# Weights cast by software-queue DMAs into place, and u transposed by DMAs on ScalarE's queue, in a fused retention and low-rank-mixer kernel

## The chip, the cores and the metric

The kernel runs on one core of one Trainium2 chip. The metric is the device time of one execution in microseconds (us); the kernel before takes 255.03 us (median of 3 runs, 253.96 to 255.19). Runs called slow (over 1.5% above the fastest of the same kernel) are left out of the ratios that are quoted.

## The reference

```python
# q, k, v: (4, 8, 768, 64); U: (768, 32); V: (32, 768); w_ch1: (512, 2048); w_ch2: (2048, 512); all fp32
state = 0                                        # per batch and head
for t in range(768):                             # retention
    state = gamma[h] * state + outer(k[t], v[t])
    y[t]  = (q[t] @ state) / 8
x  = heads of y side by side                     # (4, 768, 512)
u  = x + (x.T @ U @ V).T                         # low-rank mixing over the sequence
out = u + relu(u @ w_ch1) @ w_ch2                # MLP, "up" and "down"
```

The kernel computes the recurrence in six chunks of 128 positions, as masked scores plus a carried state ("attention" below). The MLP is nearly all of the TensorE (PE) work.

## The kernel before

The core treats batch 0's attention first and then works in four stages. In stage b the MLP of batch b runs while the attention of batch b+1, and its low-rank mixing, are woven between the MLP's matmuls at fixed marks (fractions of the MLP's work). The up half needs u transposed (uT, 512 features on partitions); the down half needs the MLP's hidden gT and w2.

```python
def prep_w1(mb, engines="PPPP"):        # w1: loaded as fp32 by SP (SyncE), cast to bf16 on POOL (GpSimd)
    for c in range(NCB):
        cast(engines[c], w1b[:, c, ts(mb, 512)], take("w1", mb, c))
        feed_more()                      # issues the next load of SP's list

def load_w2(j):                          # w2: cast by the software-queue DMA itself
    nc.gpsimd.dma_start(out=w2b[:, ds(4 * j, 4)],
        in_=moe_w_ch2[ds(512 * j, 512)].rearrange("(m p) n -> p m n", p=P))

def lr_turn(b, j0, eng="A"):             # u turned on TensorE, two blocks of 128 rows at a time
    r = R[j0 // 2 % 2]
    for c in range(NCB):
        for jj in range(2):
            nc.tensor.matmul(r[:, c // 2, ds(256 * (c % 2) + P * jj, P)],
                             us[b][:, j0 + jj, ts(c, P)], ident, start=True, stop=True)
    evac(eng, uTs[b][:, :, ds(j0 * P, 2 * P)], r.rearrange("p n (c t) -> p (n c) t", c=2))
# ... cut: attention, projection, up and down pieces ...
for ci in range(3): prep_turned("k", 1, ci)      # POOL, in this order
load_w2(0); load_w2(1)
for ci in range(3): prep_turned("q", 1, ci)
load_w2(2); load_w2(3)
# ... cut ...
AT = {1: at(0.44, 0.075, 0.037), 2: at(0.09, 0.105, 0.05)}             # attention marks
LR = {1: (0.89, 0.92, 0.945, 0.97), 2: (0.71, 0.75, 0.83, 0.89)}       # mix, expand, turn 0-1, turn 2-3
```

`evac` is an eviction: it copies the result of matmuls to the place where the next step reads it. Blocks 4 and 5 of a batch are turned early in the next stage (marks 0.06 to 0.10), because only the second part of the up half needs them. Blocks 0 to 3 are turned at the border between stages, because the very first up matmul needs all four.

Of the kernel before, what the change touches and what calls it, by code (L numbers as in the profile page):

```python
# [9 lines left out]
fp32 = mybir.dt.float32  # L10
# [6 lines left out]
def kernel(  # L17
# [11 lines left out]
    nc = tc.nc  # L29
    P = 128  # L30
    B, H, S, D = q.shape
    NCK = S // P
    DM = H * D
    RK = moe_U.shape[1]
    DH = moe_w_ch1.shape[1]
    NM = DH // P
    NCB = DM // P
# [8 lines left out]
    wts = ctx.enter_context(tc.tile_pool(name="wts", bufs=1))  # L46
    rin = ctx.enter_context(tc.tile_pool(name="rin", bufs=RING))
    rinT = ctx.enter_context(tc.tile_pool(name="rinT", bufs=1))
# [11 lines left out]
    R = [psum.tile([P, 2, 512], fp32, tag="r0", name="r0")]  # L60
# [12 lines left out]
    def evac(eng, dst, src):  # L73
        if eng == "A":
            nc.scalar.activation(dst, src, AF.Copy)  # L75
        else:
            nc.vector.tensor_copy(out=dst, in_=src)

    def cast(eng, dst, src, scale=None):
        if eng == "A":  # L80
            assert scale is None
            nc.scalar.activation(dst, src, AF.Copy)
            return
        e = nc.vector if eng == "D" else nc.gpsimd
        if scale is None:
            e.tensor_copy(out=dst, in_=src)  # L86
        else:
            e.tensor_tensor(dst, src, scale, op=ALU.mult)  # L88

    Ub = wts.tile([P, NCK, RK], bf16)  # L90
    V4 = wts.tile([P, S], bf16)
    w1b = wts.tile([P, NCB, DH], bf16)
    w2b = wts.tile([P, NM, DM], bf16)
    Vf = wts.tile([P, S], fp32)

    feed = []
    n_fed, n_used, n_held = [0], [0], [0]
# [4 lines left out]
    def feed_natural(nm, b, ci):  # L102
        src = {"q": q, "k": k, "v": v}[nm]
        feed.append(((nm, b, ci),
                     src[b, :, ts(ci, P), :].rearrange("h p d -> p h d")))
# [5 lines left out]
    def load_whole(nm, b):  # L111
        open_in(nm, b)
        src = {"q": q, "k": k}[nm][b]
        for hp in (0, 2, 1, 3):
            nc.sync.dma_start(  # L115
                out=turned_in[nm, b][ds(32 * hp, 32)].rearrange(
                    "p h c x -> p (h c) x"),
                in_=src[ds(2 * hp, 2)].rearrange("h (c t j) d -> t (h c) (j d)",
                                                 c=NCK, t=32))

    def feed_more():
        while n_fed[0] < len(feed) and n_held[0] < RING:
            key, src = feed[n_fed[0]]
            if key[0] == "T" and n_cast[key[1] - 1] < 2 * NCK:
                return
            n_fed[0] += 1
            if key[0] == "T":
                load_whole("k", key[1])
                load_whole("q", key[1])
                continue  # L130
            if key[0] == "V":
                for c in range(NCB):
                    nc.sync.dma_start(out=Vf[ds(RK * c, RK)], in_=src)
                continue
            n_held[0] += 1
            t = rin.tile([P, 512], fp32, tag="in", name=f"in_{n_fed[0]}")
            ready[key] = t
            if key[0] == "U":
                t = t[:, :NCK * RK].rearrange("p (j r) -> p j r", j=NCK)
            elif key[0] in "qkv":  # L140
                t = t.rearrange("p (h d) -> p h d", h=H)
            nc.sync.dma_start(out=t, in_=src)  # L142

    def take(*key):
        n_held[0] -= 1
        return ready.pop(key)

    for ci in range(NCK):
        for nm in "qkv":
            feed_natural(nm, 0, ci)  # L150
    feed.append((("U",), moe_U.rearrange("(j p) r -> p j r", p=P)))
    feed.append((("V",), moe_V))
    for mb in range(4):
        for c in range(NCB):
            feed.append((("w1", mb, c), moe_w_ch1[ts(c, P), ts(mb, 512)]))
    for b in range(1, B):
        feed.append((("T", b), None))
        for ci in range(NCK):
# [25 lines left out]
    for h in range(H):  # L184
        r = ds(32 * (h // 2), 32)
# [6 lines left out]
    ident = consts.tile([P, P], bf16)  # L192
# [4 lines left out]
    for i in range(NST):  # L197
        t = consts.tile([P, 4, P], bf16, name=f"state{i}")
# [34 lines left out]
            prep_natural("k", b, ci)  # L233
        prep_natural("v", b, ci)

    def prep_uv(eng):
        cast(eng, Ub.rearrange("p j r -> p (j r)"), take("U")[:, :NCK * RK])
        feed_more()
        cast(eng, V4, Vf)

    def prep_w1(mb, engines="PPPP"):
        for c in range(NCB):
            cast(engines[c], w1b[:, c, ts(mb, 512)], take("w1", mb, c))
            feed_more()

    def load_w2(j):
        nc.gpsimd.dma_start(
            out=w2b[:, ds(4 * j, 4)],
            in_=moe_w_ch2[ds(512 * j, 512)].rearrange("(m p) n -> p m n", p=P))
# [5 lines left out]
    def open_x(b):  # L255
        xs[b] = xp.tile([P, NCK, DM], bf16, tag="x", name=f"x_{b}")
# [99 lines left out]
    us, uTs, pcs = {}, {}, {}  # L356
# [27 lines left out]
                R[g][:, :, :nj * P].rearrange("p c (j e) -> p c j e", j=nj),  # L384
                v4(xs[b][:, ds(j0, nj), e]), op=ALU.add)

    def lr_turn(b, j0, eng="A"):
        r = R[j0 // 2 % 2]
        for c in range(NCB):
            for jj in range(2):  # L390
                nc.tensor.matmul(r[:, c // 2, ds(256 * (c % 2) + P * jj, P)],  # L391
                                 us[b][:, j0 + jj, ts(c, P)], ident, start=True,
                                 stop=True)
        evac(eng, uTs[b][:, :, ds(j0 * P, 2 * P)],
             r.rearrange("p n (c t) -> p (n c) t", c=2))


    stores = []

# [68 lines left out]
    def part(f, *args):  # L468
        return lambda: f(*args)


    def prep_first(ci):
        for nm, tag, g in (("q", "qi", gq), ("k", "kd", gk), ("v", "vd", None)):
            t = rpre.tile([P, H, D], bf16, tag=tag, name=f"{nm}d_0_{ci}")
            src = take(nm, 0, ci).rearrange("p (h d) -> p h d", h=H)
            if g is not None:
                g = g[:, ci, :, None].to_broadcast([P, H, D])
            cast("P", t, src, g)
            pre[nm, 0, ci] = t
            feed_more()  # L480
# [59 lines left out]
    def x_turn(j, cs):  # L540
        for c in cs:
            if c not in xT:
                xT[c] = bank("mlp" if c < 3 else "qk")
            nc.tensor.matmul(xT[c][:, ts(j, P)], xs[0][:, j, ts(c, P)], ident,
                             start=(j == 0), stop=False, skip_group_check=True)

    with tc.tile_pool(name="psum0", bufs=1, space=bass.MemoryType.PSUM) as psum0:
        open_x(0)
        prep_first(0)
        for ci in range(NCK):  # L550
            turn0(ci)
            if ci + 1 < NCK:
                prep_first(ci + 1)
            else:
                prep_uv("P")
            if ci > 0:
                mix0(ci - 1)
            score0(ci)
            if 0 < ci <= NLO:
                x_turn(ci - 1, range(3))  # L560
        n_cast[0] = 2 * NCK
        for mb in range(4):
            prep_w1(mb)
        for j in range(NLO):
            x_turn(j, (3,))
        mix0(NCK - 1)
        lr_open(0)
        p_p = bank("o")
        for j in range(NCK):
            for c in range(NCB):  # L570
                nc.tensor.matmul(p_p[ds(RK * c, RK), :P], Ub[:, j],
                                 xs[0][:, j, ts(c, P)], start=(j == 0),
                                 stop=(j == NCK - 1))
        pcs[0] = rmid.tile([P, P], bf16, tag="pc", name="pc_0")
        evac("D", pcs[0], p_p[:, :P])
        for c in range(NCB):
            nc.tensor.matmul(xT[c][:, :LO], pcs[0][ds(RK * c, RK)],
                             V4[ds(RK * c, RK), :LO], start=False, stop=True,
                             skip_group_check=True)
        for c in range(NCB):  # L580
            evac("AD"[c % 2], uTs[0][:, c, :LO], xT[c][:, :LO])
# [2 lines left out]
    R.append(psum1.tile([P, 2, 512], fp32, tag="r1", name="r1"))  # L584
    for ci in range(3):
        prep_turned("k", 1, ci)
    load_w2(0)
    load_w2(1)
    for ci in range(3):
        prep_turned("q", 1, ci)  # L590
    load_w2(2)
    load_w2(3)
    for ci in range(3):
        prep_natural("v", 1, ci)

    def at(b0, dc, dm):
        return [(b0 + dc * ci, b0 + dc * ci + dm) for ci in range(NCK)]

    AT = {1: at(0.44, 0.075, 0.037), 2: at(0.09, 0.105, 0.05)}
    LR = {1: (0.89, 0.92, 0.945, 0.97), 2: (0.71, 0.75, 0.83, 0.89)}  # L600
    for b in range(1, B):
        w = min(b, 2)
        if b > 1:
# [2 lines left out]
        else:  # L606
            marks = [(0.03, part(lr_expand, 0, 4, 2)), (0.10, part(lr_turn, 0, 4)),
                     (0.16, part(lr_expand, 0, 0, 4))]
        step = AT[w][1][0] - AT[w][0][0]
        for ci in range(NCK):  # L610
            s_at, m_at = AT[w][ci]
            marks.append((s_at - 0.6 * step, part(turn_chunk, b, ci)))
# [7 lines left out]
        def mixed():  # L620
            lr_open(b)
            lr_proj(b)
        marks += zip(LR[w], (mixed, part(lr_expand, b, 0, 4), part(lr_turn, b, 0),
                             part(lr_turn, b, 2)))
        weave(mlp_pieces(b - 1), marks)
    b = B - 1
# [32 lines left out]
```

## Time and profile before

The four stages, from the first up matmul of a batch to that of the next (from the timeline of PE):

| | first up matmul | stage 0 | stage 1 | stage 2 | stage 3 |
|---|---|---|---|---|---|
| before, us | 32.55 | 69.16 | 51.34 | 51.92 | 47.73 |

Stages 0 and 1 hold the same kinds of work, so stage 0 is about 18 us too long. The view by windows shows it, with stages 0 to 2 as its rows. The columns are the stretch, its length, then the busy time of PE, PE's weight load, DVE (VectorE), ACT (ScalarE), POOL (with instruction counts), the granted PE clock, the mean share of 16 DMA engines (it can come out above 1), and GB/s:

```profile
32.55:101.71 69.16, 59.42 (x637) 31.60 (x637) 27.63 (x49) 22.41 (x48) 34.80 (x46) 0.91 1.05 220
101.71:153.05 51.34, 51.21 (x600) 27.35 (x600) 24.65 (x45) 19.13 (x42) 27.71 (x37) 1.00 0.89 193
153.05:204.97 51.92, 51.26 (x601) 27.43 (x600) 24.98 (x45) 19.12 (x42) 13.16 (x18) 1.00 0.09 32
```

In stages 1 and 2 PE is busy almost without a gap at full clock. In stage 0 PE idles for 9.7 us and runs at a mean clock of 0.91. The table of waits of PE names the reasons (total us, times, longest):

```profile
PE r L314 <- DVE qT L264: 5.8, 1, 5.8
...
PE mlp L437 <- DMA w2b<-in_moe_w_ch_dram: 1.2, 1, 1.2
PE r L391 <- DVE u L382: 1.1, 2, 0.7
PE mlp L414 <- ACT uT L75: 0.9, 2, 0.7
```

The first line is the turned q of batch 1, which comes late from memory. The last two are what turning u on PE costs at the borders, beside the matmuls themselves. The timeline of POOL shows why w2 is late too: its DMAs stand behind casts that wait for k and q (in brackets, the idle time before and what ended it).

```profile
51.70 2.11 POOL L86 CAST ki<-kin 128x512 bf16<-128x512 f32 x3 [6.90 <-DMA kin<-in_k_dram]
53.73 1.70 POOL L247 DMA_DIRECT2D w2b<-in_moe_w_ch_dram  x2
58.52 3.04 POOL L88 TENSOR_TENSOR qi<-qin,gqT 128x512 bf16<-128x512 f32 x3 [3.10 <-DMA qin<-in_q_dram]
61.51 1.56 POOL L247 DMA_DIRECT2D w2b<-in_moe_w_ch_dram  x2
```

The border of stage 0 to 1, from the chain of waits (start, duration, what):

```profile
97.62 1.23 DVE u L382
...
99.28 0.86 PE mlp L437 x4
100.15 0.46 PE r L391 x8
...
100.63 1.03 ACT uT L75
...
101.71 1.02 PE mlp L414 x4
```

From the last piece of u (98.85) to the first matmul that uses uT (101.71) it is 2.9 us, and PE fills part of it with other work (the down matmuls, L437).

### The profile page before, as it was taken

What the parts mean: (1) busy time and instruction counts of PE and PEld (TensorE: products, weight loads), DVE (VectorE), ACT (ScalarE), POOL (GpSimd) and SP (SyncE); (2) the same over time, 40 slices, a digit from 0 to 9 for tenths busy, and PEclk for the clock granted to TensorE, in tenths of its full rate; (3) what the DMA queues carried; (4) which work ended last, traced back from release to release, by engine and by line L of the source; (5) the groups of instructions that cost most, each with busy time, mean ns of one, the idle gap of its engine ahead of it and who ended that gap; (6) DMA issues with size and microseconds to landing.
All of it is one profiled execution on the core that took longest, in us unless ns stands there. A gap on an engine that the chain in (4) does not pass through costs nothing.

```text
span 252.7 us, 5495 instructions
## 1 busy us (share of the span) xinstructions
PE 221.9 (88%) x2304; PEld 122.7 (49%) x2304; DVE 102.6 (41%) x193; ACT 87.6 (35%) x182; POOL 100.0 (40%) x138
## 2 busy tenths in 40 slices
PE   0784789954889998999999999999999999999991
PEld 0573534543545544445754454447644544584440
DVE  5433344413147434566544525556544242221121
ACT  3556335441323312555541033556410315450000
POOL 4776565057765207994108815720001010000110
PEclk9999779996599999999999999999999999999998
DMA  8999899999958999957999932000011120001211
GB/s 158 218 218 191 247 350 256 217 211 212 208 97 176 266 233 205 228 148 167 207 206 218 263 109 86 0 4 4 0 44 64 65 83 0 3 0 41 86 62 63
DMA packets 66857, 35.45 MB, mean 140 GB/s; under 512 B 51856, under 2 KB 63120, under 8 KB 66832
## 3 DMA queue, kind: packets, MB, share of 16 engines
q1 hardware_dynamic: 62800, 26.71, 52.1%
q0 software_dynamic: 4032, 8.39, 11.9%
q8 instruction: 18, 0.29, 0.5%
q14 instruction: 7, 0.06, 0.1%
HBM read 30.90 MB, written 6.29 MB: 147 GB/s over the span
## 4 chain that ended last, share of the span: by engine, by line
PE 45%; issue 20%; DMA 16%; SPq 10%; POOL 3%; DVE 2%; ACT 1%; POOLq 0%; DVEq 0%; ACTq 0%
PE mlp L437 21%; PE mlp L414 16%; SPq L142 9%; DMA in<-in_moe_w_ch_dram 5%; DMA qin<-in_q_dram 5%; DMA w2b<-in_moe_w_ch_dram 4%; PE r L347 2%; PE r L314 2%; POOL out_dram L403 2%; DMA Vf<-in_moe_V_dram 2%; SPq L115 1%; PE r L338 1%; DVE a L320 1%; PE r L391 1%; PE st L299 1%
## 5 line engine op out<-in xcount | busy, mean ns | idle before, releaser
L414 PE MATMUL mlp<-uT,w1b 128*128 128x512 bf16 (+1 forms) x512 | 92.3, 335 | 1.7 <-ACT uT L75 0.9
L437 PE MATMUL mlp<-w2b,gT 128*128 128x512 bf16 x384 | 89.5, 382 | 1.2 <-DMA w2b<-in_moe_w_ch_dram 1.2
L414 PEld LDWEIGHTS <-w1b 128*128 128x128 bf16 x512 | 49.4, 100 | 34.7 <-issue 3.7
L421 ACT ACTIVATE gT<-mlp 128x512 bf16<-128x512 f32 (+1 forms) x88 | 42.7, 490 | 53.6 <-PE mlp L414 52.7
L437 PEld LDWEIGHTS <-gT 128*128 128x128 bf16 x384 | 35.7, 98 | 40.7 <-issue 1.8
L403 POOL DMA_DIRECT2D out_dram<-o x24 | 13.3, 555 | 89.5 <-DVE o L442 89.5
L442 DVE TENSOR_TENSOR o<-mlp,u 128x512 f32<-128x512 f32 x24 | 16.6, 692 | 50.0 <-PE mlp L437 50.0
L419 DVE TENSOR_SCALAR gT<-mlp 128x512 bf16<-128x512 f32 (+1 forms) x40 | 22.0, 552 | 34.8 <-PE mlp L414 34.8
L320 DVE TENSOR_TENSOR a<-r,mask 128x512 bf16<-128x512 f32 x36 | 23.2, 685 | 18.8 <-PE r L314 17.1
L88 POOL TENSOR_TENSOR qi<-qin,gqT 128x512 bf16<-128x512 f32 x18 | 18.7, 1045 | 20.0 <-DMA qin<-in_q_dram 20.0
L75 ACT ACTIVATE x<-r 128x256 bf16<-128x256 f32 x36 | 11.8, 381 | 28.9 <-PE r L347 28.7
L88 POOL TENSOR_TENSOR vd<-in,gk 128x512 bf16<-128x512 f32 x18 | 18.7, 1043 | 7.8 <-DMA in<-in_v_dram 4.6
L75 ACT ACTIVATE uT<-r 128x1024 bf16<-128x1024 f32 x10 | 10.2, 1022 | 28.0 <-PE r L391 28.0
L86 POOL CAST ki<-kin 128x512 bf16<-128x512 f32 x18 | 13.5, 761 | 14.5 <-DMA kin<-in_k_dram 14.5
L382 DVE TENSOR_TENSOR u<-r,x 128x512 bf16<-128x512 f32 (+1 forms) x16 | 14.6, 952 | 6.6 <-PE r L375 6.6
L520 DVE TENSOR_TENSOR a<-r,mask 128x512 bf16<-128x512 f32 x12 | 7.7, 686 | 14.1 <-PE r L515 14.1
L314 PE MATMUL r<-qT,kT 32*128 32x128 bf16 x288 | 7.6, 225 | 5.8 <-DVE qT L264 5.8
L86 POOL CAST w1b<-in 128x512 bf16<-128x512 f32 x16 | 9.8, 613 | 5.5 <-DMA in<-in_moe_w_ch_dram 5.1
L314 PEld LDWEIGHTS <-kT 32*128 32x128 bf16 x288 | 4.5, 96 | 11.5 <-issue 10.3
L264 DVE STREAM_TRANSPOSE qT<-qi 128x256 f32<-128x256 f32 x18 | 7.3, 406 | 6.7 <-POOL qi L88 6.7
L489 PE MATMUL qk<-ident,qd 128*128 128x128 bf16 x24 | 3.5, 295 | 6.5 <-DVE ident L193 6.5
L75 ACT ACTIVATE qkT<-qk 128x1024 bf16<-128x1024 bf16 x6 | 6.1, 1024 | 8.7 <-PE qk L491 8.7
(70 smaller groups left out, 147.5 us busy)
## 6 DMA issues: line engine op xcount, KB each, us to landing
in<-in_v_dram SPq DMA_DIRECT2D x24, 256.0 KB, 5.7
out_dram<-o POOLq DMA_DIRECT2D x24, 256.0 KB, 2.6
in<-in_k_dram SPq DMA_DIRECT2D x18, 256.0 KB, 5.5
kin<-in_k_dram SPq DMA_DIRECT2D x12, 384.0 KB, 7.8
qin<-in_q_dram SPq DMA_DIRECT2D x12, 384.0 KB, 13.0
in<-in_moe_w_ch_dram SPq DMA_DIRECT2D x16, 256.0 KB, 6.2
w2b<-in_moe_w_ch_dram POOLq DMA_DIRECT2D x4, 512.0 KB, 9.9
in<-in_q_dram SPq DMA_DIRECT2D x6, 256.0 KB, 5.2
```

Source lines behind the costliest of these rows:

```text
L75: nc.scalar.activation(dst, src, AF.Copy)
L86: e.tensor_copy(out=dst, in_=src)
L88: e.tensor_tensor(dst, src, scale, op=ALU.mult)
L142: nc.sync.dma_start(out=t, in_=src)
L314: nc.tensor.matmul(R[hp // 2][:, hp % 2, ts(i, P)], turned("kT", b, ci, i, c, r), turned("qT", b, ci, i, c, r), start=(c == 0), stop=(c == 1))
L320: nc.vector.tensor_tensor(a[:, ds(4 * g, 4)].rearrange("p (n i) m -> p n i m", n=2), R[g][:, :, :256].rearrange("p n (i m) -> p n i m", i= ...
L403: nc.gpsimd.dma_start(out=dst, in_=src)
L414: nc.tensor.matmul(g_p[:, :sz], w1b[:, c, ts(m, P)], uTs[b][:, c, ds(lo, sz)], start=(c == 0), stop=(c == NCB - 1))
L419: nc.vector.tensor_relu(gT[:, m, ds(lo, sz)], g_p[:, :sz])
L421: nc.scalar.activation(gT[:, m, ds(lo, sz)], g_p[:, :sz], AF.Relu)
L437: nc.tensor.matmul(ch, gT[:, m, ts(j, P)], w2b[:, m], start=(m == 0), stop=(m == NM - 1))
L442: nc.vector.tensor_tensor(o_sb, ch, us[b][:, j], op=ALU.add)
```

## The change

Its intent: take the casts of w1, U and V off POOL by letting the software-queue DMA cast while it loads; load w2 early, behind w1; load k, q of batch 1 after w1 and beside w2 (a dummy POOL copy from w1's last column, the gate, holds them back); and take the transposes of u off PE and ScalarE.

```diff
-    def prep_w1(mb, engines="PPPP"): ...      (and prep_uv, Vf, the w1/U/V loads on SP)
+    def load_u():    nc.gpsimd.dma_start(out=Ub, in_=moe_U.rearrange("(j p) r -> p j r", p=P))
+    def load_v(c):   nc.gpsimd.dma_start(out=V4[ds(RK * c, RK)], in_=moe_V)
+    def load_w1(mb):
+        nc.gpsimd.dma_start(out=w1b[:, :, ts(mb, 512)],
+            in_=moe_w_ch1[:, ts(mb, 512)].rearrange("(c p) n -> p c n", p=P))
 ...
-    def lr_turn(b, j0, eng="A"):  (8 matmuls with ident, one eviction)
+    def lr_turn(b, j0):
+        for j in (j0, j0 + 1):
+            nc.scalar.dma_start(out=uTs[b][:, :, ts(j, P)], in_=us[b][:, j], transpose=True)
 ...
             turn0(ci)
             if ci + 1 < NCK:
+                if ci == NCK - 2:
+                    load_w1(0)
+                    load_w1(1)
                 prep_first(ci + 1)
+                if ci == 0:  load_u()
+                elif ci < 3: load_v(2 * ci - 2); load_v(2 * ci - 1)
 ...
+        load_w1(2); load_w1(3)
+        for j in range(4): load_w2(j)
+        gate = rinT.tile([P, 2, NCK, 256], fp32, tag="kin", name="gate")
+        nc.gpsimd.tensor_copy(out=gate[:1, 0, 0, :1], in_=w1b[:1, 0, DH - 1:])
         n_cast[0] = 2 * NCK
+        feed_more()
 ...
-    AT = {1: at(0.44, 0.075, 0.037), ...
-    LR = {1: (0.89, 0.92, 0.945, 0.97), ...
+    AT = {1: at(0.56, 0.052, 0.026), ...
+    LR = {1: (0.87, 0.89, 0.905, 0.905), ...
```

More of the change, by code (lines that the diff above doesn't have):

```diff
@@ L93 @@
     w2b = wts.tile([P, NM, DM], bf16)
-    Vf = wts.tile([P, S], fp32)
     feed = []
@@ L130, in feed_more @@
                 continue
-            if key[0] == "V":
-                for c in range(NCB):
-                    nc.sync.dma_start(out=Vf[ds(RK * c, RK)], in_=src)
-                continue
             n_held[0] += 1
@@ L137, in feed_more @@
             ready[key] = t
-            if key[0] == "U":
-                t = t[:, :NCK * RK].rearrange("p (j r) -> p j r", j=NCK)
-            elif key[0] in "qkv":
-                t = t.rearrange("p (h d) -> p h d", h=H)
-            nc.sync.dma_start(out=t, in_=src)
+            nc.sync.dma_start(out=t.rearrange("p (h d) -> p h d", h=H), in_=src)
     def take(*key):
@@ L150 @@
             feed_natural(nm, 0, ci)
-    feed.append((("U",), moe_U.rearrange("(j p) r -> p j r", p=P)))
-    feed.append((("V",), moe_V))
-    for mb in range(4):
-        for c in range(NCB):
-            feed.append((("w1", mb, c), moe_w_ch1[ts(c, P), ts(mb, 512)]))
     for b in range(1, B):
@@ L234, in prep_chunk, with load_u, load_v @@
         prep_natural("v", b, ci)
-    def prep_uv(eng):
-        cast(eng, Ub.rearrange("p j r -> p (j r)"), take("U")[:, :NCK * RK])
-        feed_more()
-        cast(eng, V4, Vf)
-    def prep_w1(mb, engines="PPPP"):
-        for c in range(NCB):
-            cast(engines[c], w1b[:, c, ts(mb, 512)], take("w1", mb, c))
-            feed_more()
+    def load_u():
+        nc.gpsimd.dma_start(out=Ub, in_=moe_U.rearrange("(j p) r -> p j r", p=P))
+    def load_v(c):
+        nc.gpsimd.dma_start(out=V4[ds(RK * c, RK)], in_=moe_V)
+    def load_w1(mb):
+        nc.gpsimd.dma_start(
+            out=w1b[:, :, ts(mb, 512)],
+            in_=moe_w_ch1[:, ts(mb, 512)].rearrange("(c p) n -> p c n", p=P))
     def load_w2(j):
@@ L385, in lr_expand @@
                 v4(xs[b][:, ds(j0, nj), e]), op=ALU.add)
-    def lr_turn(b, j0, eng="A"):
-        r = R[j0 // 2 % 2]
-        for c in range(NCB):
-            for jj in range(2):
-                nc.tensor.matmul(r[:, c // 2, ds(256 * (c % 2) + P * jj, P)],
-                                 us[b][:, j0 + jj, ts(c, P)], ident, start=True,
-                                 stop=True)
-        evac(eng, uTs[b][:, :, ds(j0 * P, 2 * P)],
-             r.rearrange("p n (c t) -> p (n c) t", c=2))
+    def lr_turn(b, j0):
+        for j in (j0, j0 + 1):
+            nc.scalar.dma_start(out=uTs[b][:, :, ts(j, P)], in_=us[b][:, j],
+                                transpose=True)
     stores = []
@@ L552 @@
             if ci + 1 < NCK:
+                if ci == NCK - 2:
+                    load_w1(0)
+                    load_w1(1)
                 prep_first(ci + 1)
-            else:
-                prep_uv("P")
+                if ci == 0:
+                    load_u()
+                elif ci < 3:
+                    load_v(2 * ci - 2)
+                    load_v(2 * ci - 1)
             if ci > 0:
@@ L560 @@
                 x_turn(ci - 1, range(3))
+        load_w1(2)
+        load_w1(3)
+        for j in range(4):
+            load_w2(j)
+        gate = rinT.tile([P, 2, NCK, 256], fp32, tag="kin", name="gate")
+        nc.gpsimd.tensor_copy(out=gate[:1, 0, 0, :1], in_=w1b[:1, 0, DH - 1:])
         n_cast[0] = 2 * NCK
-        for mb in range(4):
-            prep_w1(mb)
+        feed_more()
         for j in range(NLO):
@@ L586 @@
         prep_turned("k", 1, ci)
-    load_w2(0)
-    load_w2(1)
     for ci in range(3):
         prep_turned("q", 1, ci)
-    load_w2(2)
-    load_w2(3)
     for ci in range(3):
@@ L597, in at @@
         return [(b0 + dc * ci, b0 + dc * ci + dm) for ci in range(NCK)]
-    AT = {1: at(0.44, 0.075, 0.037), 2: at(0.09, 0.105, 0.05)}
-    LR = {1: (0.89, 0.92, 0.945, 0.97), 2: (0.71, 0.75, 0.83, 0.89)}
+    AT = {1: at(0.56, 0.052, 0.026), 2: at(0.09, 0.105, 0.05)}
+    LR = {1: (0.87, 0.89, 0.905, 0.905), 2: (0.71, 0.75, 0.83, 0.89)}
     for b in range(1, B):
```

## The prediction

> What bounds the kernel now. From about 73 us to the end TensorE sets the pace: the windows 101.7-153.2 and 153.2-204.5 hold 51.36 and 50.64 us of PE work. The first stage of MLP work (batch 0, with the attention of batch 1 woven in) is bound by loads: it lasts 32.55-101.7 us, 69.2 us, where the same mixture for the next batch takes 51.5. The 17.7 us of excess are, by the table of waits: 5.84 us for the turned q of batch 1 (POOL waits for the q load until 58.5), 0.8 us for k behind it, 1.24 us for w2 at 73.4; by the windows, PE is wholly idle from 56 to 60 and its granted clock is 0.50 from 60 to 68, which costs some 5 us more. The cause is order: w1, k, q, v share one SP queue (issues run back to back until 67 us), and POOL holds the w2 DMAs behind casts that wait for k and q (issued at 53.7 and 61.5; landing 8.5-11.3 us).
>
> What changes.
> - Removed: 18 POOL casts (w1 9.8 us, U 0.35, V 0.83), 23 SP issues; 80 TensorE transposes (0.45 us per group of 8 on the chain of waits, 10 groups, so 4.5 us) and ten 1.02 us ScalarE evictions.
> - Added: 13 POOL DMA issues (w2's took 0.76-0.93 us each), of which five fall into the batch-0 stage and two just before its last chunk; 20 DMA transposes of 128 KB on the ScalarE queue. No trace prices these. The Trainium skill ("DMA: Bandwidth & Descriptors", Latency and other measured facts) gives 261 GB/s effective for a transposing DMA, 0.5 us here; I estimate 3-4 us from issue to landing, more beside loads, and about 1 us of ScalarE's queue each.
> - Moved: all of w2 is queued right behind w1; k, q start when w1 has landed; attention of batch 1 starts at 0.56 of the MLP, not 0.44.
>
> Bytes do not fall, since the cast DMAs read fp32. The skill (same page, Issuing engines are not separate DMA queues) says all queues share 16 engines; here q beside w2 (54-64 us) moved about 205 GB/s of written bytes, or about 310 GB/s read once w2's halving is undone, w2 taking two thirds. Alone, k/q run at 215.
>
> Estimate of the first stage. The first MLP matmul comes 1-1.5 us later (33.5-34), because two w1 issues go before the last chunk's casts. w1 lands in four steps until about 40, just ahead of use; the up half ends near 57. w2 lands near 60, q near 62-65, v0 cast some 3 us later, so PE still waits, now around 59-67, with another clock dip. Then 27-28 us of work remain: the stage ends near 95.5 instead of 101.7, gain about 6. Turns off PE: 4.5 us, of which I expect half given back in waits for uT at batch borders, since all four blocks must land before the first up matmul and ScalarE's queue is blocked meanwhile. Sum: 255 - 6 - 2.5 = 246.5 us; range 240 to 251.5. Faster by over 2%: 0.73; within 2%: 0.23; slower: 0.04.
>
> What would show it: no POOL casts of w1; w2 landing by 60; the PE wait before the first batch-1 score shorter and later; stage end at 94-97; PE busy about 7 us lower; PE waiting on a transposing DMA 0.5-2 us at each of three borders; the last stage almost unchanged.
>
> What would make it wrong: transposing DMAs landing in 6 us or more, or blocking ScalarE for several us so that evictions stall PE in every up half; the software queue running far below 300 GB/s, so that w1 itself is late; on the good side, w2 and k/q overlapping to 350 GB/s, which removes the stall (240).

## The result

The changed kernel is slower: 263.57 us median (262.96 to 263.65, 4 runs) against 254.50 us; ratio 1.035, 95% interval 1.031 to 1.039. A ratio here is the mean time of one kernel's fast runs over the mean of the other's in the same rounds, so it is not quite the ratio of the medians quoted beside it. The prediction (246.5, range 240 to 251.5, 4% for slower) is wrong in its sign.

Stages 0 to 2 after, by windows:

```profile
35.24:104.51 69.27, 56.64 (x613) 29.39 (x612) 28.10 (x49) 19.44 (x45) 20.79 (x26) 0.95 0.99 188
104.51:157.80 53.29, 51.93 (x577) 26.39 (x577) 23.70 (x43) 15.97 (x39) 27.99 (x36) 0.97 0.86 169
157.80:213.22 55.42, 51.52 (x576) 26.62 (x577) 25.56 (x46) 16.05 (x39) 16.57 (x24) 0.97 0.37 90
```

Every term of the loss can be placed: the start is 2.7 us later, stage 0 is as long as before although its loads were meant to shorten it, stage 1 is 2.0 us longer, stage 2 3.5 us, stage 3 0.9 us. PE's busy time in stages 1 and 2 did not fall although 48 transposing matmuls (24 in each stage) are gone from them: the granted clock is 0.97 instead of 1.00, and slower matmuls count as more busy time. PE's waits now:

```profile
PE mlp L395 <- DMA uT<-u: 12.5, 3, 7.2
PE mlp L395 <- DVE o L423: 2.4, 1, 2.4
PE r L301 <- DVE qT L251: 0.9, 1, 0.9
```

The third line does not lie in stage 0, as the timeline of PE shows:

```profile
166.58 0.62 PE L301 MATMUL r<-qT,kT 32*128 32x128 bf16 x16 [0.85 <-DVE qT L251]
```

So in stage 0 the waits for q (5.8 us before) and for w2 are gone, as intended. In their place PE waits 12.5 us for transposing DMAs: 4.26 us at 52 to 56, 7.20 us at the border of stage 0 to 1, and 1.06 us at the next border. At the last border it does not wait for them. What the trace says of these DMAs (the columns of the first line: engine's queue, count, issue time min/median/max in ns, first and last start):

```profile
L376 ACTq DMA_TRANSPOSE uT<-u x20: 1205/1286/1306, 42.3 to 218.5; - x20
DMA to landing us min/median/max: 2.4/3.1/12.6
```

Each holds ScalarE's queue for 1.29 us (median), and lands between 2.4 and 12.6 us after its issue. The border, from the chain of waits, which answers to the lines shown of before:

```profile
94.06 1.22 DVE u L369
...
99.20 5.17 DMA uT<-u
104.37 0.14 issue
104.51 1.86 PE mlp L395 x4
```

u is complete at 95.3, and the first matmul that uses uT starts at 104.5: 9.2 us where PE and ScalarE took 2.9. The timeline of ScalarE (start, duration, what) shows what lies between:

```profile
95.31 5.18 ACTq L376 DMA_TRANSPOSE uT<-u  x4
```

Four issues run one after the other, 5.18 us in all, the last of them from 97.88 to 99.16 us (chain); then the last DMA takes another 5.2 us to land. The last line of the chain shows a second price: the first four matmuls take 1.86 us, before it was 1.02, since PE had been idle. The Trainium skill ("TensorE: Matmul & The Clock Gate", Part 1) says that about 3.4 us without work puts the array at half clock; both traces agree (here 7.2 us of idling; in the kernel before, clock 0.50 from 60 to 68 us after an idle stretch of 5.8 us). Here shorter gaps did it too: after gaps of 2.39 and 0.85 us in stage 2 the clock was 0.61 and 0.54 in the two stretches of 2 us from 165.8 us on, so these runs do not show 3.4 us as a threshold.

One more line surprised me, in the table of waits of SP, which only issues loads:

```profile
SPq L133 <- DMA uT<-u: 40.1, 10, 11.6
```

Loads of v and k, which have no data in common with uT, wait 40 us in total (10 times, the longest 11.6 us) for transposes. The built program explains it: every DMA issued from SP or ScalarE takes the next of eight completion semaphores in turn (counters that a DMA raises when its data have landed), and a DMA may be issued only when the last user of its semaphore has landed. The two queues share the eight.

### The profile page after: what moved, and what is told of

It is laid out like the page before. It is cut to its first block, busy times and chain, and to the rows that moved or that the text cites. A ratio compares the mean times of both kernels' runs of the same rounds, so it can differ in the third digit from the quotient of the medians.

```text
span 261.8 us, 5299 instructions
## 1 busy us (share of the span) xinstructions
PE 224.0 (86%) x2224; PEld 120.4 (46%) x2224; DVE 102.6 (39%) x193; ACT 77.5 (30%) x172; POOL 95.1 (36%) x130
## 4 chain that ended last, share of the span: by engine, by line
PE 33%; issue 31%; DMA 13%; SPq 6%; DVE 6%; POOL 6%; ACTq 3%; ACT 1%; POOLq 0%; DVEq 0%
PE mlp L395 15%; PE mlp L418 10%; DMA uT<-u 8%; SPq L133 6%; DMA in<-in_v_dram 4%; ACTq L376 3%; POOL out_dram L384 2%; DVE u L369 2%; PE r L334 2%; DMA out_dram<-o 2%; PE r L301 2%; DVE a L307 1%; PE r L325 1%; POOL vd L88 1%; PE st L286 1%
## 5 line engine op out<-in xcount | busy, mean ns | idle before, releaser
L395 PE MATMUL mlp<-uT,w1b 128*128 128x512 bf16 (+1 forms) x512 | 94.6, 341 | 17.3 <-DMA uT<-u 12.5
L418 PE MATMUL mlp<-w2b,gT 128*128 128x512 bf16 x384 | 88.0, 380 | 0.0
L395 PEld LDWEIGHTS <-w1b 128*128 128x128 bf16 x512 | 50.2, 101 | 54.0 <-issue 17.7
L418 PEld LDWEIGHTS <-gT 128*128 128x128 bf16 x384 | 35.5, 98 | 40.1
L75 ACT ACTIVATE qkT<-qk 128x1024 bf16<-128x1024 bf16 x6 | 6.1, 1024 | 10.8 <-PE qk L472 10.8
L86 POOL CAST kd<-in 128x512 bf16<-128x512 f32 x12 | 7.3, 610 | 4.2 <-DMA in<-in_k_dram 3.9
L251 DVE STREAM_TRANSPOSE kT<-ki 128x256 f32<-128x256 f32 x18 | 7.8, 436 | 0.0
L88 POOL TENSOR_TENSOR qd<-in,gq 128x512 bf16<-128x512 f32 x6 | 6.3, 1058 | 3.2 <-DMA in<-in_q_dram 3.2
```

The lines of the kernel that those rows point to most:

```text
L75: nc.scalar.activation(dst, src, AF.Copy)
L86: e.tensor_copy(out=dst, in_=src)
L88: e.tensor_tensor(dst, src, scale, op=ALU.mult)
L395: nc.tensor.matmul(g_p[:, :sz], w1b[:, c, ts(m, P)], uTs[b][:, c, ds(lo, sz)], start=(c == 0), stop=(c == NCB - 1))
L418: nc.tensor.matmul(ch, gT[:, m, ts(j, P)], w2b[:, m], start=(m == 0), stop=(m == NM - 1))
```

## The experiments

The theory after the result: the loads are a gain, and the DMA transposes lose it and more, by three routes: (a) matmuls wait for uT; (b) ScalarE's queue is held; (c) loads on SP are held or slowed by the transposes. The rival: the new load order is the loss (later start, late q), and the transposes only show it. Stage lengths from the profile of each kernel that the next three sections compare, in us. The one with border 0-1 on PE is left out, because its profiled run was a slow one.

| kernel | first up matmul | stage 0 | stage 1 | stage 2 | stage 3 |
|---|---|---|---|---|---|
| before | 32.55 | 69.16 | 51.34 | 51.92 | 47.73 |
| after | 35.24 | 69.27 | 53.29 | 55.42 | 48.58 |
| loads only | 35.26 | 61.98 | 51.35 | 51.91 | 48.10 |
| turns only | 32.62 | 75.37 | 53.63 | 56.35 | 48.23 |
| after, first turn on PE | 34.77 | 67.84 | 53.33 | 55.38 | 48.58 |
| after, border 1-2 on PE | 34.99 | 69.36 | 53.07 | 50.59 | 48.59 |
| loads only + unread transposes | 35.11 | 67.30 | 52.56 | 54.34 | 48.99 |
| loads only + unread copies | 35.31 | 65.89 | 51.34 | 52.53 | 48.13 |
| loads only + tiny unread copies | 35.18 | 61.91 | 51.35 | 52.35 | 48.11 |
| loads only + busy ScalarE | 34.99 | 62.18 | 54.83 | 52.82 | 48.88 |

### Each half of the change alone

Loads only: the changed kernel with the turns of u on PE again and the old border marks.

```diff
-        for j in (j0, j0 + 1):
-            nc.scalar.dma_start(out=uTs[b][:, :, ts(j, P)], in_=us[b][:, j], transpose=True)
+        (the eight matmuls and the eviction of the kernel before)
-    LR = {1: (0.87, 0.89, 0.905, 0.905), ...
+    LR = {1: (0.89, 0.92, 0.945, 0.97), ...
```

> The change's loads (cast DMAs, k/q behind w1, attention of batch 1 from 0.56) with the turns of u back on TensorE. Theory (the loads are a gain, the DMA turns the loss): 248 to 251 us, stage of batch 0 ends near 96-98 instead of 101.7, SP never waits on a transpose. Rival (the new load order itself is the loss, through the later first MLP matmul and late q): 256 us or more.

Measured 250.85 us (250.39 to 251.47) against 254.87; ratio 0.984, interval 0.977 to 0.991. A hit for the theory. The start is 2.7 us later, stage 0 7.2 us shorter, and stages 1 and 2 are the same as before to 0.01 us.

Turns only: the kernel before with the DMA transposes and the new border marks, which were not tried apart from each other.

> The kernel before with only the DMA turns (and their marks 0.87/0.89/0.905/0.905). Theory: the turns alone lose 8 to 13 us, so 263 to 268 us, with PE waiting several us on a transposing DMA at the border of batch 0 to 1. Rival (new loads are the loss): within 2 us of 254.5, about 252 if the 4.5 us of PE work are really saved.

Measured 269.20 us (267.96 to 269.55); ratio 1.054, interval 1.048 to 1.061, a little worse than expected. So the halves are -4.0 and +14.3 us, together +10.3; the whole change measured +9.1 (263.57 less 254.50). They nearly add up, and the rival falls: the load order is not the loss.

### Which transposes cost

First turn on PE (`if b > 0:` before the DMA form):

> The changed kernel with only the first turn (batch 0, last two blocks) on TensorE. Theory (that transpose lands 12.6 us late because it runs beside k, q and w2, and PE waits 4.3 us for it): PE no longer waits at 52-56 us; 2 to 5 us faster than after, 259 to 261.5. Rival (the wait only hides the wait for q behind it): the gain shows up as a longer wait for q, total within 1 us of after.

Measured 262.01 us, ratio 1.027, 1.6 us less than after. Neither side was quite right: the wait of 4.26 us is gone, but a wait of 3.40 us for q has come up in stage 0, where the changed kernel had none. Most of the wait for uT had only hidden the wait for q.

```profile
64.81 0.40 PE L301 MATMUL r<-qT,kT 32*128 32x128 bf16 x16 [3.40 <-DVE qT L251]
```

Border 0-1 on PE (the four transposes of batch 1's blocks 0 to 3 as matmuls):

> The changed kernel with only the four transposes at the border of batch 0 to 1 on TensorE. Theory (issue of 4 x 1.29 us plus landing beside the loads of batch 2 costs the 7.2 us wait and a clock dip): that wait goes, 7 to 10 us faster than after, 253.5 to 256.5. Rival (PE would wait there anyway, for example for k, q of the next batch): gain under 3 us.

Measured 256.35, 257.94 and 254.89 us in the three fast runs and 259.80 in a slow one, so a mean of 256.4 us for the fast ones: 7.2 us below after, at the lower edge of what was expected. The runs scatter more than others; the sign is safe, the tenth is not.

Border 1-2 on PE:

> The changed kernel with only the four turns at the border of batch 1 to 2 on TensorE. There the chain of waits runs transpose, v load held behind it, POOL's scaling of v, the stores queued behind that, the output eviction, PE (2.4 us) although the tiny copies showed that the shared semaphores alone cost nothing. If that chain is real: SP issues the last loads of batch 3 before 150 us instead of 162, the wait for the output eviction goes, the third stage takes 52 to 53 us instead of 55.4 and the total is 2.5 to 4.5 us under after. If ScalarE's blocked queue in the up half (the fifth and sixth block) is what costs there: the third stage stays at 54 or more.

Measured 258.72 us (258.38 to 259.69), 4.9 us below after, more than expected. Stage 2 fell from 55.42 to 50.59, which is also 1.3 us below loads-only (51.91): no load runs in this stage, and the difference fits the three groups of 0.45 us that its three DMA turns take off PE. This stage 2 had no large direct wait. The chain of waits of the changed kernel, in extracts, shows how a transpose reached PE through four other engines and queues:

```profile
146.59 2.36 DVE u L369 x2
...
148.97 2.43 DMA uT<-u
...
151.41 3.20 DMA in<-in_v_dram
...
154.75 1.04 POOL vd L88
155.79 0.53 POOL out_dram L384
...
159.58 4.26 DMA out_dram<-o
...
163.96 0.69 DVE o L423
164.65 1.20 DVE u L369 x2
```

The transpose is issued only when u is there; a v load of batch 3, with the same semaphore, waits for it to land; POOL waits for v and has output stores queued behind it; the output buffers stay taken, so DVE's eviction waits, and PE with it (2.39 us, and 0.85 us behind that for DVE's transposes of q). With the border on PE, SP issued its last load at 150.4 us instead of 162.2, and the waits of DVE for stores and of PE for DVE are gone. The run takes away the holding, the direct wait of 1.06 us and the issues together, so the 4.8 us are not split further, but the three named waits (2.39, 0.85 and 1.06 us) make 4.3 of them.

### Without any reader

Unread transposes: the loads-only kernel, PE turning u, and 20 transposes issued as well, into a scratch tile.

```diff
+    def unread_turn(b, j0, n=2):
+        for j in range(j0, j0 + n):
+            scr = xp.tile([P, NCB, P], bf16, tag="scr", name=f"scr_{b}_{j}", bufs=4)
+            nc.scalar.dma_start(out=scr, in_=xs[b][:, j], transpose=True)
+    # called right after each turn of blocks 4-5; two calls more at 0.865 (stage 0), or at 0.80 and 0.86 (others)
```

> The loads-only kernel (turns on TensorE), with the change's 20 transposing DMAs issued as well, into a tile that nobody reads, near the places of the changed kernel. No matmul can wait for them. Theory (the turns lose time in three ways: matmuls wait for uT, ScalarE's queue is held 1.29 us each, and loads on SP wait for transposes because both queues share eight completion semaphores): 253 to 258 us against 250.9 for loads-only, SP still waits 25 us or more in total on transposes, the natural loads of batch 3 still come after 150 us and PE still waits on an output eviction early in the third stage. Rival (only the direct waits for uT cost): within 1 us of 250.9.

Measured 259.78 us (258.68 to 260.20), 8.9 us above loads-only: more than the theory allowed, and the rival is dead. Twenty transposes cost that much although no matmul waits for them. Stage 0 is 5.3 us longer because q comes later. PE's wait for it in loads-only (first) and here:

```profile
PE r L301 <- DVE qT L251: 2.7, 1, 2.7
```

```profile
PE r L301 <- DVE qT L251: 6.8, 1, 6.8
```

Stages 1 to 3 are 4.5 us longer together. As expected, SP waits 33 us in total for the transposes, and the last six natural loads of batch 3 (k and v as they lie in memory) come after 150 us. PE does not wait on an output eviction itself, but in stage 2 it waits 1.16 us for a piece of u that DVE could only add after an eviction held up 4.79 us by stores. That is the chain of the changed kernel once more. PE's other new waits are for evictions of the up half by ScalarE, 2.7 us in stages 1 to 3. One of the first kind and two of the second:

```profile
159.59 0.40 PE L378 MATMUL r<-ident,u 128*128 128x128 bf16 x4 [0.96 <-DVE u L369]
164.59 1.02 PE L405 MATMUL mlp<-uT,w1b 128*128 128x512 bf16 x4 [0.74 <-ACT gT L412]
109.39 1.89 PE L405 MATMUL mlp<-uT,w1b 128*128 128x512 bf16 x8 [1.16 <-ACT gT L412]
```

These 8.9 us must not be added to the direct waits of the changed kernel. In its stage 0 PE idles for 12.6 us, of which 11.5 are direct waits for uT, and it does not wait for q at all: the late q hides behind the late uT.

Three more runs replace the unread transpose by something that has only part of it.

Plain copies of the same 128 KB (`in_=xs[b][:, j]` into the same tile, without `transpose=True`):

> As the kernel with unread transposes (259.8), but each transposing DMA made a plain copy of the same 128 KB; the same completion semaphores, the same places. If the transposing (some 544 small packets each, landing up to 13 us beside loads, 1.29 us of issue) is what costs: 251 to 253.5 us, copies land in 2 to 4 us also beside loads. If any 128 KB DMA on ScalarE's queue does it, through the shared semaphores alone: 257 us or more.

Measured 254.79 us (254.19 to 254.96), between the two answers. By the profiles stage 0 is 3.9 us longer than in loads-only, again with a late q (PE waits 5.6 us for it), and stage 2 is 0.6 us longer. Landing times of the transposes (first line) and of the copies (second), from the views of the scratch tile in the two kernels:

```profile
DMA to landing us min/median/max: 2.4/3.3/13.2
```

```profile
DMA to landing us min/median/max: 2.0/3.6/7.3
```

The DMA table of the two pages gives the packets of ScalarE's queue (packets, MB, share of 16 engines' time):

```profile
q10 hardware_dynamic: 10880, 2.62, 7.1%
```

```profile
q10 hardware_dynamic: 2880, 2.62, 3.6%
```

Same bytes, 544 packets for each transpose against 144 for a copy, twice the engines' time, and 1.8 times the longest landing.

Tiny copies (512 bytes each, same semaphores, same order):

> The same with 512 bytes in each unread copy: no bytes to speak of, little issue, only the shared semaphores and their order remain. If loads on SP lose mainly because they may not be issued before a DMA of ScalarE's queue has been issued and has landed, at whatever size: 253 us or more, with SP waiting over 10 us in total on these copies. If the semaphores cost only through the slow landing of the transposes: within 1 us of loads-only, 250 to 252.

Measured 251.40 us (250.02 to 252.15), within 1 us of loads-only. SP still waits 21 us in total on them, the longest time 7.0 us, and it costs nothing that these totals show. Shared semaphores alone are not the loss. They pass a delay on when the DMA before them is late by more than the loads can spare, as in stage 2 of the changed kernel, where the longest hold was 11.6 us.

Busy ScalarE (an ordinary ScalarE copy of 128x1280 elements, 1.27 us, in place of each unread transpose):

> The loads-only kernel with a ScalarE copy of about 1.2 us in place of each unread transpose: ScalarE's time alone, no DMA. Theory (it is the small part): 251 to 253 us, all of it in the up halves where evictions wait behind two copies. Rival (ScalarE's blocked queue is most of the 9 us): 256 us or more.

Two of four runs were slow; the fast ones took 255.51 and 256.43 us. That is about 5 us over loads-only, so my "small part" was wrong, though two runs are few. The profile (of a fast run) puts 5.2 us into stages 1 to 3, where the unread transposes put 4.5. The sums agree, but in part by luck. Here 3.5 us fall in stage 1: two copies in a row delay the evictions of the up half, PE stalls for 1.77 us, and its clock is 0.55 and 0.59 in the next two stretches of 2 us.

```profile
104.76 3.00 PE L406 MATMUL mlp<-uT,w1b 128*128 128x512 bf16 x8 [1.77 <-ACT gT L413]
```

With unread transposes the clock stays at 1.00 in stages 1 and 2, and more than half of the loss (2.4 us) falls in stage 2, partly through the late loads. So ScalarE's held queue is shown to be one cause in stages 1 to 3, and not the whole of it; in stage 0 it costs nothing (62.18 against 61.98).

### What makes a transpose slow

The first turn earlier (marks 0.0 and 0.03 instead of 0.03 and 0.10):

> The changed kernel with the first turn moved from 0.10 to 0.03 of the first MLP, so that it is issued about 36.5-38 us, before k and q start. Theory (k and q beside it, and w2, make it take 12.6 us where a quiet one takes 2.4): landing in 3 to 6 us, PE no longer waits at 52 us, total 1 to 3 us less than after, as with that turn on TensorE (262.0). Rival (the cast DMAs alone slow it so, or it is slow in itself): landing stays at 9 us or more.

Measured 262.04 us (2 runs). The transposes were issued at 39.9 us, not before 38, because the whole stage starts at 36.2; k had begun at 39.3, so the run did not do what it was made for, and the landing stayed at 13.3 us. Inconclusive, so made again in another way: first turn issued before the MLP, and k, q released only by its landing (the gate reads uT in place of w1).

> The changed kernel with the first turn issued ahead of the MLP and k, q of batch 1 released only when it has landed, so that only the cast DMAs of w1 and w2 run beside it. If the many loads of k and q on SP's queue make it land after 12.6 us: it lands in 2.5 to 5 us. If the cast DMAs do: 8 us or more. In between: both. The total is not at issue (k, q start later).

From the chain of waits of that kernel:

```profile
38.79 10.49 DMA uT<-u
```

The second transpose lands after 10.5 us with nothing but the cast DMAs of w1 and w2 beside it, so k and q are not needed to make it slow. (One run, 267.93 us; its total is not at issue.) But the cast DMAs are not needed either. In the turns-only kernel SP loads w1 plainly and the first w2 DMA is issued only at 51.8 us. Its first two transposes, issued at 40.1 and 41.5 us beside plain loads alone, landed after 9.4 and 10.5 us (the longest of the kernel):

```profile
L389 ACTq DMA_TRANSPOSE uT<-u x20: 1205/1286/1417, 40.1 to 223.3; - x20
DMA to landing us min/median/max: 2.4/3.1/10.5
L247 POOL DMA_DIRECT2D w2b<-in_moe_w_ch_dram x4: 760/793/922, 51.8 to 64.8; - x4
```

So heavy loads of either kind do it, and the slow landing is not something that the two halves of the change do to each other. The packets in the traces show one thing that goes with it: beside loads mostly in packets of 1 KB (w1, w2, turned k and q) the transposes landed after 8.4 to 13.3 us, at the border of stage 0 to 1, beside loads mostly in packets of 256 bytes, after at most 5.7 us, and beside output stores at most after 2.4 to 3.7 us. No run changed the packets alone. The skill ("DMA: Bandwidth & Descriptors", Queues, rings and completion order) says that an engine takes turns between queues packet by packet. 544 small packets that take turns with packets of 1 KB fit such a picture, but no run here shows the turns themselves.

The border with loads held back (batch 2's loads released by the border's last transpose but the marks unchanged; preparation of batch 2 moved behind that):

> The changed kernel with all loads of batch 2 held until the four transposes at the border of batch 0 to 1 have landed, so that these run with no load beside them. Splits the 7.2 us wait into issue and contention. Theory: each lands 2.4-2.7 us after its issue and the wait shrinks to 4 to 5 us, what four issues of 1.29 us and one quiet landing leave. Rival (contention is most of it): wait under 2.5 us; other rival (contention is nothing): wait stays at 6.5 us or more. The total is not at issue; the held loads will cost more later.

```profile
94.64 1.28 ACTq L379
95.93 0.04 issue
95.97 2.50 DMA uT<-u
98.47 0.14 issue
98.61 1.44 PE mlp L398 x3
```

A hit: the last one lands after 2.5 us instead of 5.2, and PE's wait is 4.54 us instead of 7.20. So of the border's wait some 2.7 us were contention; the rest is four issues in a row and one landing, and stays when no load runs. (Whether earlier marks would hide more of it was not tried at this border. At the two later borders of the changed kernel the marks lie further from the end of the stage, at 0.83 and 0.89, and PE waited 1.06 us at one and not at all at the other.) (A single run, 273.87 us because the held loads come late, as intended; its first loads happened to run faster than in other runs, so I read only the border.)

### A version that beats both

Loads only has PE wait 2.7 us for q. Release k and q at half of w1 (`in_=w1b[:1, 0, 1023:1024]` in the gate):

> Loads-only kernel with k and q of batch 1 let go when the second quarter of w1 has landed instead of the last (about 34 instead of 40 us). If the wait for q (2.7 us at 62-65) limits the stage of batch 0: q lands about 60, that wait goes, 1.5 to 3 us less than loads-only, 248 to 249.5. If w2 or w1 is pushed back as much by it: no gain, or a new wait for w1 or w2, 250.5 or more.

Measured 249.32 us (248.70 to 249.79), ratio 0.977, interval 0.971 to 0.983: a small gain as expected, though PE still waits 2.05 us for q.

The same with U, V issued first and w1 only after the last chunk's casts:

> The loads-only kernel with k and q released at half of w1, and with U and V issued on POOL before the first chunk (POOL is idle there until 4 us) and w1 only after the last chunk's casts. The first MLP matmul came 2.7 us later than in the kernel before, because these issues (3.1 + 1.6 us) stand between POOL's casts. Expected: first MLP matmul at 33 to 34, total 247 to 248.5 us. If the later w1 or the wait for q takes it back: 249 or more.

Measured 253.77 us: a clear miss. The first up matmul did come 1.3 us earlier (33.78), but w1 landed later, and so the gate opened later and q with it; PE waited 7.1 us for q. What limits stage 0 is the arrival of q, not the start of the MLP.

Release at a quarter of w1, and the same with U, V first but w1 in its old place:

> The loads-only kernel with k and q released when the first quarter of w1 has landed (half: 249.3). If the arrival of q limits the stage of batch 0: wait for q under 1 us, 247 to 248.5. If w1 or w2 then come late: a wait for them, 249.5 or more.

> The same, with U and V issued first on POOL and w1 left where it is (the version with w1 moved behind the last casts lost 4.5 us to a late q). Expected: first MLP matmul at 33.5 to 34.5, total 246 to 248. If U and V only push the loads of batch 0 back by as much: as the quarter kernel.

Measured 250.07 us (0.979) and 249.39 us (three fast runs of four, 0.974), both above what I expected. The start hardly moved (34.8 and 35.1 us), and no step past "half" can be told from it. A repeat with five rounds:

> A repeat of the quarter kernel with early U and V, with five rounds, beside the next one: 248 to 250 us, ratio to before 0.970 to 0.982.

249.78 us (247.61 to 251.21), ratio 0.985, outside the range I gave for it: stage 0 varies by a few us from run to run here.

At last, DMA transposes only at the border of stage 2 to 3, where no load runs:

```diff
+        if b == B - 1 and j0 < 4:
+            for j in (j0, j0 + 1):
+                nc.scalar.dma_start(out=uTs[b][:, :, ts(j, P)], in_=us[b][:, j], transpose=True)
+            return
```

> The same, with only the four transposes of the border of batch 2 to 3 by DMA, where no load runs (they landed in 2.4 us there, and no matmul waited). Theory (a DMA turn pays where the queues are quiet and the matmuls have room): the third stage, 51.9 us, becomes 50.4 to 51, total 0.8 to 1.8 us less than the same kernel without them. Rival (a DMA turn costs even there): equal or slower.

248.65 us (248.26 to 249.28), ratio 0.979, interval 0.976 to 0.982; 1.1 us less than the repeat beside it by the medians. The run-to-run spread of that repeat is wider than this, so the total alone doesn't settle it. The stage does: it is 51.91 to 51.93 us in every kernel with PE turns and no extra DMAs, and 51.03 here, with no wait for uT. That is 0.9 us, the two turns of 0.45 us that left PE, just short of the 0.9 to 1.5 that I expected. By its median it is the fastest version, about 2% below before; by the ratio (0.979) it cannot be told from the one with the gate at half (0.977).

## Why the prediction was wrong

Right, point by point:
- The reading of stage 0 (bound by loads; q, w2, clock) and its remedy. Loads alone measure -4.0 us, where I had -6; the stage ends at 97.24 us in the loads-only kernel, where I had 95.5. In the changed kernel w1 landed by 40.2 us (predicted 40) and q by 65.1 (predicted 62 to 65); in loads-only by 39.1 and 63.3.
- That the last stage would hardly change (47.73 to 48.58).
- That the transposes would be waited for at borders (though 0.5 to 2 us at each of three became 7.20, 1.06 and nothing, with 4.26 more inside stage 0), and issue would cost about 1 us (1.29).

Mis-sized in the loads' part: the first up matmul came at 35.24, not 33.5 to 34. The DMA issues for U (1.01 us), for V (two pairs, 1.05 and 1.04) and for the first half of w1 (a pair, 1.61) stand between POOL's casts.

The step that failed is "Turns off PE: 4.5 us, of which I expect half given back in waits for uT at batch borders", together with the estimate "3-4 us from issue to landing, more beside loads". The term was to be -2.3 us. It measured +12.7 us (263.57 less 250.85) on top of loads-only, +14.3 on top of before. What the runs showed in its place:
1. The 4.5 us of PE time are real, but only a quiet place yields them: 0.9 us were had at the border of stage 2 to 3 alone, and 1.3 us in stage 2 of the kernel with border 1-2 on PE, both without loads.
2. Latency, not throughput, is what a border needs. I looked at 0.5 us of transfer; the chain is four issues of 1.29 us in a row, then a landing of 2.4 us at best: 7.6 us or more, against 2.9 us by PE and ScalarE. The quiet-border run shows 4.54 us of wait that stay when the loads are held back, and contention adds 2.7. In stage 0 of the changed kernel the direct waits for uT make 11.5 of PE's 12.6 us of idle time.
3. The landing "more beside loads" was 12.6 us for the first turn, beside cast DMAs, k and q. Cast DMAs alone (10.5 us) and plain loads alone (10.5 us, turns only) are each enough, so the new loads are not to blame: the turns cost 14.3 us without them and 12.7 with them.
4. There are indirect costs, which I did not count at all: unread transposes alone cost 8.9 us. In stage 0 they delay q (5.3 us; plain copies of the same bytes 3.9 us, tiny ones nothing); in the changed kernel this overlaps with the direct waits. In stages 1 to 3 (4.5 us) PE waits 2.7 us more for evictions behind ScalarE's held queue and 1.2 us for the late loads of point 5.
5. In stage 2 the late transposes held back loads with the same semaphore, and through POOL, stores and DVE they reached PE.

I also expected PE's busy time to fall by 7 us. It rose from 221.9 to 224.0: the idle stretches put PE at half clock, and slow matmuls are longer. My list of what would make the prediction wrong did contain "landing in 6 us or more, or blocking ScalarE for several us"; I gave it too little weight, having no trace of such a DMA.

What stays open: how the indirect 5.3 us of stage 0 split between the slower q and the fewer loads that may be outstanding at once; the scatter of stage 0 from run to run in the later versions; why transposes land late beside loads in large packets; and whether earlier border marks would have hidden the wait of 7.2 us.

## What to carry to other kernels

Before work is moved from an engine to a DMA, compare latencies at the place where the result is awaited (issue times the number of DMAs, plus the landing beside the traffic that will be there), not busy times. Ask what else the new DMA holds: the queue of the engine that issues it, the other queues' completion semaphores, and the loads that are on the critical path. When a change has two halves, run each alone first: here one was worth -4 us and the other +14.

## What the Trainium skill lacked or had wrong

- "DMA: Bandwidth & Descriptors", Latency and other measured facts, gives a transposing DMA 261 GB/s; for 128 KB that makes 0.5 us, as an estimate. It gives no latency for a small one from on-chip memory to on-chip memory, and no page that I read says how much later it lands beside loads. ("VectorE: DVE Perf Modes", The three transpose paths, has one time, 1309 ns for 128x128 by the DMA.) Here, for 128 KB: 1.29 us of issue and 2.4 us to landing when quiet, up to 13.3 us beside loads.
- The same page, Issuing engines are not separate DMA queues, says that several issuing engines only save issue time "which is usually small relative to the DMA itself". For a 128 KB transpose it is not small: 1.29 us of issue against 2.4 us to landing, and it holds up ScalarE's other work (2.7 us of PE's waits with unread transposes).
- "Advanced Engine Details and Errata", X-Bar Transpose, says that transpose DMAs are as fast as regular ones. Quiet, that nearly holds (2.4 against 2.0 us at best for the same 128 KB); beside loads it doesn't: up to 13.2 against 7.3 us, with 544 packets against 144 and 7.1% against 3.6% of the DMA engines' time.
- No page that I read warns that DMAs of two issuing engines may share completion semaphores in a built program, so that loads wait for another engine's DMA (40 us in total here), nor when it matters (holds up to 7.0 us cost nothing, one of 11.6 us did).
